# Ranks of the last masks and the places of the last transposes in a two-layer attention and MLP kernel

## Chip, cores and metric

The kernel runs on one core of one Trainium2 chip. The metric is the device time of one execution in microseconds, as the median of several runs. The engines are named as in the profile: PE is TensorE, DVE is VectorE, ACT is ScalarE, POOL is GpSimd, SP is SyncE, which here only issues DMAs.

## What is computed

One sequence of 2048 rows and 640 columns goes twice through the same pair of layers: causal attention with a sliding window of 256 over 32 heads of 20 columns, then an MLP of width 1536 with a squared relu. All is in float32.

```python
def _A_ref(x, wqkv, wo):                      # H = 32, Dh = 20, W = 256
    qkv = ((x @ wqkv).reshape(B, S, 3, H, Dh)).transpose(2, 0, 3, 1, 4)
    q, k, v = qkv[0], qkv[1], qkv[2]
    scores = jnp.einsum("bhqd,bhkd->bhqk", q, k) * (Dh ** -0.5)
    mask = (idx[:, None] - idx[None, :] >= 0) & (idx[:, None] - idx[None, :] < W)
    p = _softmax(jnp.where(mask[None, None], scores, -1e9), axis=-1)
    o = jnp.einsum("bhqk,bhkd->bhqd", p, v)
    return o.transpose(0, 2, 1, 3).reshape(B, S, D) @ wo

def _B_ref(x, w1, b1, w2, b2):                # F = 1536
    h = jnp.einsum("bsd,df->bsf", x, w1) + b1
    r = jnp.where(h > zero, h, zero)
    return jnp.einsum("bsf,fd->bsd", r * r, w2) + b2

x = A_x
x = x + _A_ref(_layernorm(x), A_wqkv, A_wo);  x = x + _B_ref(_layernorm(x), B_w1, B_b1, B_w2, B_b2)
x = x + _A_ref(_layernorm(x), A_wqkv, A_wo);  x = x + _B_ref(_layernorm(x), B_w1, B_b1, B_w2, B_b2)
```

## The kernel before

The rows are cut into units of 256 (two blocks of 128), eight per layer, so sixteen units `u` = 0 to 15 over both layers. Precision comes from splitting operands into a high and a low float16 half: every product of `mm3` runs three matmuls per slice of 128 of the contraction (high by high, high by low, low by high) into one PSUM accumulation.

The heads of a unit are worked in eight groups of four; group `n` counts over all units, so unit 15 has the groups 120 to 127. For each group there are these steps. `max_quad` computes scores for the row maxima, two groups and more ahead. `exp_quad` computes the scores again, transposed, into the six banks of the two `bb` tiles (matmuls at L757); ACT takes six exponentials of them (L779), and POOL sets to zero what lies outside the window with eight masks (`affine_select`, L794 and L798). `pv_quad` multiplies by the values (L828) in three steps, each of which needs its own masks, and ACT copies the result out (L840).

Beside the groups runs the dense work of a neighbouring unit: `stage_qk`, `stage_v`, `stage_o` (the product with `wo`), `stage_y` (normalized rows are transposed by TensorE and evicted as two halves, ACT's cast at L377 and DVE's subtraction at L378) and `stage_f` (the MLP). `stage_f` has a first half of six pairs of tiles of `w1`: a relu on ACT (L1003), a square on POOL (L1007), a cast on ACT (L1010) and a subtraction on DVE (L1013) give the two halves of `hh`. Four buffers hold the relu's output. Its second half has, for each block of rows, chunks of 36 matmuls over `w2`, each ended by an add on DVE (L1042) and, at the end of a block, a store. The accumulations of the dense work take turns in two PSUM banks (`mm_tile`). `load_o` brings the attention's output back from DRAM and divides it by the row sums (`od`, L904 to L914).

The order of the instructions on every engine is written out when the program is built, by a small planner inside the kernel. The dense work is a generator that yields after some 500 ns of matmuls (a piece), with the cost that the kernel assumes for them; `step` advances a clock `now` by that cost. Work for the other engines is posted as jobs with an assumed cost, dependences and a rank `prio`. `post` keeps the list sorted by rank, and within a rank in the order of posting. `pump` takes, again and again, the first job of the list that is ready and can start within `LOOK` = 250 ns of the clock (or another one of the same engine that fits in before it), and emits it. The assumed costs decide only the order; on the chip each engine runs its instructions in that order and waits for semaphores.

Before the change, a mask has rank 1 and a square rank 0, so of two that are due the square is emitted first. In unit 15 the dense work beside the groups is that of unit 14, and the first half of its MLP lies beside the groups 124 to 126. The last lines of the kernel then run the rest: `some(dense, 10e3)` runs pieces of unit 14's MLP for at least 10e3 ns of assumed cost and on to the end of a chunk (until no bank holds an unfinished accumulation), `stage_o(15)` follows, `some(dense, 4e3)` runs the last chunk, and `stage_y(15)` transposes both blocks, five transposes each, into `bb`. Then comes `stage_f(15)`, the last MLP, which has TensorE for itself.

Of the kernel before, what the change touches and what calls it, by code (L numbers as in the profile page):

```python
# [26 lines left out]
NU = NL * NG  # L27
# [4 lines left out]
NQ = H // 4  # L32
# [13 lines left out]
def kernel(ctx: ExitStack, tc: tile.TileContext, x, wqkv, wo, w1, b1, w2, b2, out):  # L46
# [86 lines left out]
    def post(eng, cost, fn, *deps, wait=0.0, prio=1, **kw):  # L133

        j = Job(eng, cost, fn, [d for d in deps if d is not None], now[0] + wait, prio, **kw)
        k = len(pend)
        while k and pend[k - 1].prio > prio:
            k -= 1
        pend.insert(k, j)
        return j  # L140
# [457 lines left out]
    def banks():  # L598
        need(*bbjobs)
        bbjobs.clear()  # L600
        return bb6

    def quarters(u):

        return u % NG != 0
# [131 lines left out]
    def exp_quad(n):  # L737

        u, qd = divmod(n, NQ)
        qt = qts[u]  # L740
        bb = banks()
        whole = not quarters(u) or n == NQ
        steps = steps_of(u)
        if qd % GQ == 0:
            need(rowjobs.pop((u, qd // GQ)))
        pieces = []
        for k, st in enumerate(steps):
            o = 0
            for kb, kt, ko, q0, qn in st:
                w = qn * P  # L750
                for j in range(2):
                    for h in range(0 if whole else 2):
                        a, b = (0, w - 64 * (1 - h)) if kb < 2 else (64 * h, w)

                        def put(e, k=k, kt=kt, ko=ko, q0=q0, j=j, h=h, o=o, a=a, b=b):
                            r, rows = slice(64 * e, 64 * e + 3 * DH + 2), slice(64 * h, 64 * (h + 1))
                            nc.tensor.matmul(bb[e][rows, k, o + a:o + b],  # L757
                                             kt[r, 2 * qd + j, ko + 64 * h:ko + 64 * (h + 1)],
                                             qt[r, 2 * qd + j, q0 * P + a:q0 * P + b], start=True, stop=True,
                                             tile_position=(64 * e, 64 * h))  # L760

                        pieces.append((h, b - a, put))
                    for e in range(2 if whole else 0):
                        r = slice(64 * e, 64 * e + 3 * DH + 2)
                        nc.tensor.matmul(bb[e][:, k, o:o + w], kt[r, 2 * qd + j, ko:ko + P],
                                         qt[r, 2 * qd + j, q0 * P:q0 * P + w], start=True, stop=True)
                    o += w
        by_tiles(pieces)
        now[0] += (870.0 if whole else 763.0) if u % NG else 530.0
        out, masks = [], []  # L770
        for k, st in enumerate(steps):
            pts, ms = [], []
            for e in range(2):
                o = sum(2 * qn * P for _, _, _, _, qn in st)
                box = {}

                def power(k=k, e=e, o=o, box=box):
                    box["pt"] = sb.tile([P, 512], F32, name="pt", tag="pt", bufs=6)
                    nc.scalar.activation(box["pt"][:, :o], bb[e][:, k, :o], AF.Exp, scale=SCALE / (QS * QS))  # L779

                ex = post("A", 50 + 0.834 * o, power, prio=urgency["turn"])
                bbjobs.append(ex)
                o2 = 0
                for kb, kt, ko, q0, qn in st:
                    w = qn * P
                    part = slice(o2, o2 + 2 * w)
                    o2 += 2 * w

                    def mask(box=box, part=part, kb=kb, w=w):
                        pj = box["pt"][:, part].rearrange("p (j n) -> p j n", j=2)  # L790
                        if kb < 2:

                            m = pj[:, :, w - P:w]
                            nc.gpsimd.affine_select(out=m, in_=m, pattern=[[0, 2], [-1, P]],  # L794
                                                    compare_op=ALU.is_gt, fill=0.0, base=0, channel_multiplier=1)
                        else:
                            m = pj[:, :, 0:P]
                            nc.gpsimd.affine_select(out=m, in_=m, pattern=[[0, 2], [1, P]],  # L798
                                                    compare_op=ALU.is_ge, fill=0.0, base=0, channel_multiplier=-1)

                    ms.append(post("G", 375, mask, ex))
                    pts.append((e, kb, q0, qn, box, part))
            out.append(pts)
            masks.append(ms)
        return out, masks
# [168 lines left out]
    def stage_y(u, *between):  # L974

        y2s[u] = y2 = sb.tile([P, 2, KC, T], F16, name="y2", tag="qd", bufs=1)
        ypre[u] = []
        bb = banks() if u == NU - 1 else (None, None)
        for i in range(2):
            y, j = ys.pop((u, i))  # L980
            yield from split_t(y, y2[:, :, :, i * P:(i + 1) * P], j, ypre[u], bb[i])
            for g in between[i:i + 1]:
                yield from g
# [76 lines left out]
    def run(*gs):  # L1060
        s = Stream(chain(*gs))
        while not s.over:
            if s.go() is None and not s.over:
                wait_any(s.want)
# [19 lines left out]
    def some(dense, cost):  # L1084

        while cost > 0 or not all(banks2):
            c = next(dense, None)
            if c is None:
                break
            if not isinstance(c, Want):  # L1090
                cost -= c
            yield c

    def together(ns, ms, dense, cost, share=1.0, whole=True, after=None, pace=0):

        ts = list(turns(ns, ms, pace))
        total = sum(t[0] for t in ts)
        done = part = 0.0
        quad = None
        s = Stream(dense)  # L1100

        def work(part, w):

            nonlocal done
            while True:
                t = when(w) if w else None
                ready = t is not None and t <= now[0]
                if done >= cost * share * part / total and (ready or not w):
                    return
                c = s.go()  # L1110
                if c is not None:
                    done += c
                elif ready or (s.over and not w):
                    return
                else:
                    wait_any(*([w] if w else []), *([s.want] if s.want else []))

        for k, (part_, what, m) in enumerate(ts):
            kind = what and what[0]
            wants = list(bbjobs)  # L1120
            if kind == "s" and what[1] % GQ == 0:
                wants.append(rowjobs[what[1] // NQ, what[1] % NQ // GQ])
            if m is not None:
                wants += [trips[m // NQ, j, m % NQ] for j in range(2)]
            if kind == "v":
                wants += quad[1][0]
            work(part, Want(*wants, bank=kind == "v"))
            if kind == "s":
                quad = exp_quad(what[1])
                for it in late:  # L1130
                    max_out(*it)
                late.clear()
            if m is not None:
                max_quad(m)
                if m % GQ == GQ - 1:
                    if m // NQ > 1:
                        max_cross(m // NQ, m % NQ // GQ)
                    else:
                        late.append((m // NQ, m % NQ // GQ))
            if kind == "v":  # L1140
                pv_quad(what[1], quad)
            if after and k == 0:
                after()
            part += part_
            if what is None:
                work(part, None)
                for it in late:
                    max_out(*it)
                late.clear()
        work(part, None)  # L1150
        if whole:
            while not s.over:
                if s.go() is None and not s.over:
                    wait_any(s.want)
# [73 lines left out]
    while not all(j.end is not None and j.end <= now[0] + LOOK for j in bbjobs):  # L1228
        c = next(rest)
# [5 lines left out]
    for u in range(1, NU):  # L1235
        last = u == NU - 1
        quads, ahead = range(NQ * u, NQ * (u + 1)), range(NQ * u + LEAD, NQ * (u + 1) + LEAD)
        parts, cost, ahead_ln = [], OC + FCST, u + 2 if u + 2 < NU else None
# [10 lines left out]
        dense = chain(*parts, stage_f(u - 1, ahead_ln))  # L1249
        share = 1.0 - KEEP / cost if last else 1.0 - CARRY / cost if u == NU - 2 else 1.0  # L1250
        together(quads, ahead, dense, cost, share, u < NU - 2, after=(lambda: load_o(u - 1, last)) if u > 1 else None, pace=NQ)
    load_o(NU - 1, True)
    run(some(dense, 10e3), stage_o(NU - 1), some(dense, 4e3))
    run(stage_y(NU - 1, iter(()), dense), stage_f(NU - 1))
    need(*list(pend))


# [26 lines left out]
```

## Time and profile before

| what | value |
|---|---|
| median of 3 runs | 1587.85 us (1587.21 to 1589.04) |
| the profiled execution's time | 1588.33 us |
| its span, from the first to the last instruction | 1586.6 us |
| granted TensorE clock, mean | 0.995 |
| busy: PE, DVE, ACT, POOL | 98%, 62%, 46%, 38% |

The span is what the profile's rows add up to. The execution's time is 1.73 us longer and the median of the runs lies 0.48 us under it. Times in the rows count from the span's start. A row of the timeline reads: start, length, engine, line, operation, output and inputs with their shapes, the count of instructions, and in brackets the idle time of the engine ahead of them with what ended it. A row of the chain of waits reads: start, length, engine, tile and line.

### The profile page before, as it was taken

What the parts mean: (1) busy time and instruction counts of PE and PEld (TensorE: products, weight loads), DVE (VectorE), ACT (ScalarE), POOL (GpSimd) and SP (SyncE); (2) the same over time, 40 slices, a digit from 0 to 9 for tenths busy, and PEclk for the clock granted to TensorE, in tenths of its full rate; (3) what the DMA queues carried; (4) which work ended last, traced back from release to release, by engine and by line L of the source; (5) the groups of instructions that cost most, each with busy time, mean ns of one, the idle gap of its engine ahead of it and who ended that gap; (6) DMA issues with size and microseconds to landing.
All of it is one profiled execution on the core that took longest, in us unless ns stands there. A gap on an engine that the chain in (4) does not pass through costs nothing. (4 is left out here: it accounts for less than half of the span.)

```text
span 1586.6 us, 52541 instructions
## 1 busy us (share of the span) xinstructions
PE 1558.1 (98%) x21570; PEld 1168.7 (74%) x21570; DVE 984.7 (62%) x3254; ACT 734.3 (46%) x1593; POOL 600.3 (38%) x1291
## 2 busy tenths in 40 slices
PE   8899999999999999999999999999999999999989
PEld 7666777777777777777777777777778777676767
DVE  8776665666756656565566656657665666756532
ACT  4455545444454444535443453444535345354512
POOL 1233534235253443524324252442525325254512
PEclk9998999999999999999999999999999999999999
DMA  9764343362533525354352534535343343431020
GB/s 272 191 181 117 77 107 86 96 131 55 122 87 103 111 57 127 78 124 90 91 132 64 121 87 110 104 70 128 68 125 83 97 111 69 114 87 58 29 67 18
DMA packets 243353, 160.44 MB, mean 101 GB/s; under 512 B 91176, under 2 KB 226856, under 8 KB 243112
## 3 DMA queue, kind: packets, MB, share of 16 engines
q1 hardware_dynamic: 236744, 147.58, 38.8%
q10 hardware_dynamic: 6368, 9.50, 2.1%
q8 instruction: 169, 2.77, 0.7%
q14 instruction: 72, 0.59, 0.1%
HBM read 84.68 MB, written 52.95 MB: 87 GB/s over the span
## 5 line engine op out<-in xcount | busy, mean ns | idle before, releaser
L779 ACT ACTIVATE pt<-bb 128x512 f32<-128x512 f32 (+1 forms) x736 | 376.0, 600 | 227.0 <-PE bb L757 197.8
L633 DVE CUSTOM_DVE_ANT_0 bb<-bb,maskq 128x320 f32<-128x320 f32 x896 | 409.2, 524 | 86.8 <-PE bb L653 74.6
L794 POOL TENSOR_SCALAR_AFFINE_SELECT pt<-pt 128x256 f32<-128x256 f32 x448 | 188.0, 422 | 563.1 <-ACT pt L779 550.3
L327 PE MATMUL acc<-y,w_s 128*128 128x256 f16 x2880 | 328.3, 273 | 2.5 <-ACT y L377 1.4
L327 PE MATMUL acc<-w_s,hh 128*128 128x320 f16 (+1 forms) x2340 | 326.1, 297 | 0.0
L327 PEld LDWEIGHTS <-w_s 128*128 128x128 f16 x2880 | 276.5, 98 | 54.4 <-issue 18.1
L327 PEld LDWEIGHTS <-hh 128*128 128x128 f16 x2340 | 222.1, 98 | 96.8 <-issue 11.5
L327 PEld LDWEIGHTS <-wq_s 128*128 128x128 f16 x2400 | 229.9, 98 | 46.3 <-issue 13.5
L327 PE MATMUL acc<-yT,wq_s 128*128 128x256 f16 x2250 | 258.6, 273 | 2.2 <-DVE qd L510 0.8
L798 POOL TENSOR_SCALAR_AFFINE_SELECT pt<-pt 128x256 f32<-128x256 f32 x512 | 213.7, 439 | 93.0 <-ACT pt L779 91.6
L1013 DVE TENSOR_TENSOR hh<-r,hh 128x256 f16<-128x256 f32 x192 | 95.1, 517 | 208.8 <-ACT hh L1010 201.8
L828 PE MATMUL pv<-pt,vt 128*32 128x128 f32 (+1 forms) x3840 | 190.9, 331 | 1.2 <-POOL pt L798 1.2
L1007 POOL TENSOR_TENSOR r<-r 128x256 f32<-128x256 f32 x192 | 114.2, 615 | 161.2 <-ACT r L1003 158.8
L840 ACT COPY ot<-pv 128x256 f32<-128x256 f32 x128 | 47.7, 373 | 268.8 <-PE pv L828 268.7
L327 PE MATMUL acc<-wo_s,od 128*128 128x320 f16 x960 | 141.7, 303 | 4.8 <-ACT od L911 3.0
L633 DVE DVE_READ_ACCUMULATOR2_ANT mx<- 128x1 f32 x1024 | 145.1, 142 | 0.0
L828 PEld LDWEIGHTS pv<-pt,vt 128*32 128x32 f32 x3840 | 105.4, 110 | 41.7 <-POOL pt L798 6.5
L327 PE MATMUL acc<-wq_s,yT 128*128 128x320 f16 x900 | 132.0, 299 | 1.4 <-DVE y L378 0.9
L327 PEld LDWEIGHTS <-od 128*128 128x128 f16 x960 | 92.1, 99 | 51.0 <-issue 6.4
L1003 ACT ACTIVATE r<-acc,b1s 128x256 f32<-128x256 f32 x192 | 80.7, 472 | 87.7 <-PE acc L327 86.4
L327 PEld LDWEIGHTS <-yT 128*128 128x128 f16 x900 | 85.7, 98 | 39.3 <-issue 6.7
L364 POOL TENSOR_TENSOR bmv<-bmv,neghalf 128x1 f32<-128x1 f32 x64 | 45.5, 717 | 136.1 <-DVE bmv L358 135.7
(95 smaller groups left out, 1226.3 us busy)
## 6 DMA issues: line engine op xcount, KB each, us to landing
qt<-qk SPq DMA_DIRECT2D x30, 480.0 KB
kt<-qk SPq DMA_DIRECT2D x30, 480.0 KB
qk<-qd SPq DMA_DIRECT2D x17, 640.0 KB
o<-ot SPq DMA_DIRECT2D x256, 42.0 KB
od<-o SPq DMA_DIRECT2D x14, 640.0 KB
qk<-yl SPq DMA_DIRECT2D x13, 640.0 KB
qk<-qd SPq DMA_DIRECT2D x17, 320.0 KB
xt<-in_A_x_dram SPq DMA_DIRECT2D x16, 320.0 KB
```

The costliest lines, as they stand in the source:

```text
L327: nc.tensor.matmul(acc, lhs(a, c), rhs(b, c), start=(k == 0), stop=(k == 3 * nk - 1))
L364: j = post("G", 520, lambda: nc.gpsimd.tensor_tensor(box["mv"][:, 3:4], box["mv"][:, 2:3], neghalf, op=ALU.pow), j, prio=prio)
L633: nc.vector.tensor_tensor_reduce(out=v, in0=v, in1=mask, scale=1.0, scalar=-3.0e38, op0=ALU.add, op1=ALU.max, accum_out=accum[e, w]),
L779: nc.scalar.activation(box["pt"][:, :o], bb[e][:, k, :o], AF.Exp, scale=SCALE / (QS * QS))
L794: nc.gpsimd.affine_select(out=m, in_=m, pattern=[[0, 2], [-1, P]], compare_op=ALU.is_gt, fill=0.0, base=0, channel_multiplier=1)
L798: nc.gpsimd.affine_select(out=m, in_=m, pattern=[[0, 2], [1, P]], compare_op=ALU.is_ge, fill=0.0, base=0, channel_multiplier=-1)
L828: nc.tensor.matmul(pv[32 * jj:32 * (jj + 1), q0 * P:(q0 + qn) * P], vf[:, c:c + 32], pj[:, j, :], start=(k == 0), stop=(k == len(steps) - ...
L840: nc.scalar.copy(ot[:, qd % 2], pv)
L1003: nc.scalar.activation(box["r"], acc[:, f, :], AF.Relu, bias=b1s[:, f0 + f:f0 + f + 1], scale=1.0 / (YS * WS))
L1007: nc.gpsimd.tensor_tensor(box["r"], box["r"], box["r"], op=ALU.mult)
L1013: nc.vector.tensor_sub(hh[:, 1, f, :], box["r"], hh[:, 0, f, :])
```

## The change

The masks of the groups 125, 126 and 127 are posted with rank 0, the squares' rank, instead of 1. The last chunk of unit 14's MLP is cut: a new function `portion` runs pieces until their assumed cost is used up, whether an accumulation is finished or not. After `stage_o(15)` come pieces for 1.8e3 ns, then the transposes of block 0, then pieces for 1.6e3 ns, then the transposes of block 1, then what is left of the chunk, and then `stage_f(15)`. Before, the whole chunk came first, then the transposes of both blocks. No arithmetic is changed.

```diff
-                    ms.append(post("G", 375, mask, ex))
+                    ms.append(post("G", 375, mask, ex, prio=0 if n > NQ * NU - 4 else 1))
...
     def some(dense, cost):
 
         while cost > 0 or not all(banks2):
+            c = next(dense, None)
+            if c is None:
+                break
+            if not isinstance(c, Want):
+                cost -= c
+            yield c
+
+    def portion(dense, cost):
+
+        while cost > 0:
             c = next(dense, None)
             if c is None:
                 break
...
     load_o(NU - 1, True)
-    run(some(dense, 10e3), stage_o(NU - 1), some(dense, 4e3))
-    run(stage_y(NU - 1, iter(()), dense), stage_f(NU - 1))
+    run(some(dense, 10e3), stage_o(NU - 1), portion(dense, 1.8e3))
+    run(stage_y(NU - 1, portion(dense, 1.6e3), dense), stage_f(NU - 1))
     need(*list(pend))
```

## The prediction

> **What bounds the kernel now.** I read the page first, then the chain of waits over the last 107 us, which is where the diff acts: groups 125 to 127 of the last attention unit and the last MLP.
>
> ```profile
> span 1586.6 us, 52541 instructions
> ...
> PE 1558.1 (98%) x21570; PEld 1168.7 (74%) x21570; DVE 984.7 (62%) x3254; ACT 734.3 (46%) x1593; POOL 600.3 (38%) x1291
> ...
> 1496.34 1.95 PE pv L828 x32
> ...
> 1506.91 1.34 POOL r L1007 x2
> 1508.25 0.60 POOL pt L798
> ...
> 1508.89 0.63 PE pv L828 x6
> ...
> 1513.58 1.44 PE pv L828 x32
> ...
> 1526.57 0.49 DVE kt L1042
> 1527.06 0.81 DVE od L914 x2
> ...
> 1541.44 0.49 ACT y L377
> ...
> 1541.95 0.57 DVE y L378
> ...
> 1542.54 1.04 ACT y L377 x3
> ...
> 1544.22 39.37 PE acc L327 x359
> ```
>
> TensorE is busy for 98% of the span, so almost nothing but its holes can be won, and the chain leaves TensorE (the rows that are not PE) in three places after 1500 us. Around 1506 to 1508.9 it goes through ACT's relu, two squares on POOL and one mask on POOL (L798): `pv` of group 126 waits for its last mask, which stands behind two squares. At 1526.6 it goes through DVE's add and `od`. At 1541.4 to 1544.2 it goes through ACT's and DVE's evictions of the transposes (L377, L378). The diff touches the first and the third. The views of single engines show the sizes:
>
> ```profile
> 1506.23 1.49 PE L828 MATMUL pv<-pt,vt 128*32 128x256 f32 x26
> 1508.89 0.63 PE L828 MATMUL pv<-pt,vt 128*32 128x256 f32 x6 [1.18 <-POOL pt L798]
> 1509.46 0.75 PE L757 MATMUL bb<-qt,kt 62*64 62x192 f16 x32
> ...
> 1535.80 5.05 PE L327 MATMUL acc<-w_s,hh 128*128 128x320 f16 x36
> 1540.69 1.26 PE L391 MATMUL bb<-ident,xt 128*128 128x128 f32 x10
> 1543.35 0.27 PE L327 MATMUL acc<-y,w_s 128*128 128x256 f16 x1 [1.40 <-ACT y L377]
> 1544.22 1.03 PE L327 MATMUL acc<-y,w_s 128*128 128x256 f16 x8 [0.60 <-DVE y L378]
> ```
>
> From the first transpose (1540.69) to the second matmul of the last MLP (1544.22) pass 3.53 us, though the ten transposes and one matmul need about 1.2.
>
> **The masks, part by part.** The edit adds and removes no instruction: in groups 125 to 127 eight masks each get rank 0 instead of 1 in the planner's list, so that among POOL jobs due at one moment the one posted first goes first, not the square.
>
> ```profile
> 1492.76 1.37 POOL L794 TENSOR_SCALAR_AFFINE_SELECT pt<-pt 128x256 f32<-128x256 f32 x3 [1.07 <-ACT pt L779]
> 1494.27 1.18 POOL L1007 TENSOR_TENSOR r<-r 128x256 f32<-128x256 f32 x2
> 1495.40 0.41 POOL L798 TENSOR_SCALAR_AFFINE_SELECT pt<-pt 128x256 f32<-128x256 f32 x1
> ...
> 1496.12 1.49 POOL L798 TENSOR_SCALAR_AFFINE_SELECT pt<-pt 128x256 f32<-128x256 f32 x3
> ...
> 1505.83 0.76 POOL L798 TENSOR_SCALAR_AFFINE_SELECT pt<-pt 128x256 f32<-128x256 f32 x2
> 1506.91 1.34 POOL L1007 TENSOR_TENSOR r<-r 128x256 f32<-128x256 f32 x2 [0.31 <-ACT r L1003]
> 1508.21 0.63 POOL L798 TENSOR_SCALAR_AFFINE_SELECT pt<-pt 128x256 f32<-128x256 f32 x1
> ...
> 1513.08 1.12 POOL L798 TENSOR_SCALAR_AFFINE_SELECT pt<-pt 128x256 f32<-128x256 f32 x3
> ```
>
> ```profile
> 1496.34 1.01 DVE L1013 TENSOR_TENSOR hh<-r,hh 128x256 f16<-128x256 f32 x2 [3.75 <-ACT hh L1010]
> ...
> 1506.17 1.03 DVE L1013 TENSOR_TENSOR hh<-r,hh 128x256 f16<-128x256 f32 x2 [4.55 <-ACT hh L1010]
> ```
>
> The planner's clock settles order only, never a time here. Its constants are those of the code, in ns: exponential 477, relu 360, square 571, mask 375, 165 from the end of a job on ACT to one that needs it; a job is put in order once it can start within 250 of the clock, the lower rank first.
>
> *Group 126.* Before the last step of `pv` the planner needs mask 8. Counted from the end of the scores, eight dense pieces of 545 and two steps of `pv` of 480 put its clock at 5320. The first pair's relu starts after two pieces, its squares at 1090 + 360 + 165 = 1615, five masks follow, and mask 7 ends at 1615 + 2 x 571 + 5 x 375 = 4632. The second pair's relu starts after eight pieces, its square at 4360 + 360 + 165 = 4885. So mask 8 and that square are both due; today the square's rank puts both squares first, after the change mask 8 goes first. Earlier nothing flips: after four pieces (2180), when the second square is put, mask 3 can't start before 1090 + 720 + 477 + 165 = 2452, 272 off and not within 250. So POOL runs mask 8 straight behind mask 7: the two masks at 1505.83 take 0.76, so it starts at about 1506.55 and ends after 0.41 (the mask at 1495.40) to 0.63 (the row at 1508.21), at 1506.96 to 1507.18, not 1508.84. An unbroken `pv` takes 1.44 in the chain (group 127); group 126 spans 1509.46 - 1506.23 = 3.23, to the start of the scores of 127. Gain: 3.23 - 1.44 = 1.79 at most. Its last six matmuls last 1509.46 - 1508.89 = 0.57 up to those scores, so mask 8 is due at 1506.23 + 1.44 - 0.57 = 1507.10, and its later end costs 0.1. I take **1.7**.
>
> A subtraction on DVE (L1013, x2, 1506.17 to 1507.20) runs beside that mask. Beside such subtractions the three masks at 1496.12 took 1.49, against 0.41 for one alone and 0.76 for two; so a mask is stretched by about 0.2, which the 1507.18 holds. Were it to wait out the subtraction instead, it would run from 1507.20 to 1507.61, 0.5 late, and the gain would be 1.3 (rival 3). [...] The three masks at 1496.12 speak for a stretch: with two waits of 0.4 each they would have taken 2.0 instead of 1.49.
>
> *Group 125.* The fourth mask goes ahead of the two squares (today: after them, 1495.40). The second square still goes before mask 5, by the same 272 ns. POOL's work is the same, but between mask 3 and the first square it idles about 0.14 (1492.76 + 1.37 = 1494.13 to 1494.27), which mask 4 now fills. `pv` of 125 takes 1.95 instead of 1.44; from these 0.51 the last mask wins at least 0.14 and at most all. I take **0.2**: POOL stays the limit.
>
> *Group 127.* No squares compete with its masks, but the last two squares now end about 0.2 later while the scores come 1.7 earlier, so their casts to `hh` come before the exponentials on ACT:
>
> ```profile
> 1507.71 0.40 ACT L1010 CAST hh<-r 128x256 f16<-128x256 f32 x1 [0.52 <-POOL r L1007]
> ...
> 1510.31 3.04 ACT L779 ACTIVATE pt<-bb 128x512 f32<-128x512 f32 x6 [0.33 <-PE bb L757]
> ```
>
> Scores start at 1507.7; six exponentials start 0.85 after their scores now (1509.46 to 1510.31), that would be 1508.5. The second square ends at about 1508.3, its cast takes 0.41 and ends at 1508.9, so exponentials and masks come 0.36 late. The masks end at 1513.08 + 1.12 = 1514.20 and `pv` needs the last at about 1513.58 + 1.44 - 0.57 = 1514.4, a slack of 0.2 that the 0.36 overdraws. **-0.2**; ends 0 and -0.4. The number of dense pieces between scores and `pv` stays (six pieces of four matmuls, 24): they wait for the planned end of the exponentials, which moves with the scores. The `od` wait at 1526.6 also stays: its cover, 84 matmuls after `pv`, is the same.
>
> Masks together: 0.2 + 1.7 - 0.2 = 1.7, ends 1.0 and 2.3.
>
> **The transposes, part by part.** The edit moves matmuls of the last chunk of the previous MLP (36 at 0.136, from 5.05 less the tail of 0.16). A piece is four matmuls of 136 by the code, 544 ns: 1.8e3 takes four pieces (16 matmuls), 1.6e3 three (12), 8 are left. The transposes' bank is `bb`, the chunk's a `mm` bank, so nothing has to be finished first. Beside the 0.136 no switching cost shows: the first transpose begins at 1540.69 = 1535.80 + 36 x 0.136, and ten take 1.1 without their tail. Two more switches I bound at 0 to 0.1 each.
>
> The normalized rows must be ready:
>
> ```profile
> 1534.37 0.60 DVE L366 TENSOR_SCALAR xt<-x,bmv 128x640 f32<-128x640 f32 x1
> ...
> 1538.38 0.61 DVE L366 TENSOR_SCALAR xt<-x,bmv 128x640 f32<-128x640 f32 x1 [0.66 <-POOL bmv L364]
> ...
> 1543.60 0.89 DVE L378 TENSOR_TENSOR y<-bb,y 128x384 f16<-128x384 f32 x2 [0.23 <-ACT y L377]
> ...
> 1541.44 0.48 ACT L377 CAST y<-bb 128x384 f16<-128x384 f32 x1 [10.17 <-PE bb L391]
> ...
> 1541.86 0.37 SPq L952 DMA_DIRECT2D xt<-in_B_b_dram  x1
> ```
>
> `y` of block 0 ends at 1534.97, of block 1 at 1538.99. In the old clock, new order: 16 matmuls to 1537.98; five transposes (0.55) to 1538.53; 12 matmuls to 1540.16; five transposes to 1540.71; 8 matmuls to 1541.80. Block 1 has 1.2 us of slack. On DVE, block 1's normalization is planned before block 0's subtraction, so it isn't delayed. Eviction of block 1, by today's intervals: ACT starts 0.75 after the first transpose (1540.69 to 1541.44): 1540.91; 0.48 and then 0.57 on DVE (the chain's first) end at 1541.97. The first matmul may start at 1541.80, the second at 1542.0 instead of 1544.22: **2.2**. The second half (256 columns for 384, so about two thirds of 0.48 and of 0.57) ends at about 1542.7; the eleventh matmul, the first that asks for it whole, comes at 1541.8 + 1.2 = 1543.0 (0.109 each: eight span 1.03 in the row at 1544.22, one 0.27). Ends: 2.3, if nothing waits; 1.0, if ACT's copy gets its signal only behind the eight matmuls that follow.
>
> What else moves: the chunk's add on DVE and its store now come after the second evictions, at about 1542, and free a bank that the MLP asks for 3.3 us later. The load of `b2` (SP, 1541.86 now) needs only block 0's buffer and is planned ahead of that store; even behind it, at 1542.5, it lands some 0.6 later than now while POOL's squares are due 2.2 earlier. That delays squares by up to 1.5 us, against the two pairs (6.5 us) that pass before a relu needs their buffer. No cost. After that the 39.37 us of TensorE are the same.
>
> **Sum.** 1.7 + 2.2 = 3.9 us. The profiled execution's span is 1586.6 and its time 1588.33; that becomes 1584.4. The median of the runs, 1587.85, lies 0.48 under it, and becomes **1584.0**.
>
> **Rivals.**
> 1. *The ranks do nothing, or what they give is lost at once* (the planner's order differs from my working, or group 127 loses what 126 wins): the transposes alone, 1587.85 - 2.2 = 1585.7. Against it: both jobs are due by hundreds of ns, only the rank decides. 0.11.
> 2. *The evictions still come last.* A signal behind the eight matmuls, or DVE's add ahead of the subtraction, leaves 1.0 or less of the transposes: 1587.85 - 1.7 - 0.8 = 1585.4. For it: ACT's second copy waits for DVE today (1542.54), so these two engines take turns for a reason that isn't in the source. 0.09.
> 3. *The mask waits out the subtraction* rather than being stretched: gain in 126 is 1.3, so 1587.85 - 3.5 = 1584.4. 0.10.
> 4. *Slower: masks that wait for exponentials hold up the squares.* POOL works in order. If a whole group of masks went before a pair of squares, relus would run out of their four buffers. The squares at 1494.27 have until the relu two pairs later:
>
> ```profile
> 1503.06 0.84 ACT L1003 ACTIVATE r<-acc,b1s 128x256 f32<-128x256 f32 x2
> ```
>
> With subtractions done at about 1497.4, that is 5.7 us of slack; only a delay beyond it costs. Held behind group 126's last mask (1508.84) the squares, casts and subtractions end at about 1510.9, and that relu is 7.9 us late; net of the transposes' 2.2 the time is 1593.6. Against it: the planner keeps every job within 250 ns of its clock, so a square waits for a mask or two. 0.05.
>
> **How the numbers follow.** Forecast 0.62, rivals 0.11, 0.09, 0.10, 0.05, and 0.03 unnamed. 0.2% (3.2 us, about what a measurement of this kernel can tell from no change) lies inside the forecast's reach: with terms of 1.0 to 2.3 and 2.0 to 2.3, about one in eight of its cases wins less. Faster by over 0.2%: 0.55 of the forecast's 0.62, 0.08 of rival 3, 0.01 unnamed, 0.64. Slower: rival 4 and 0.01, 0.06. Same: 0.30. The range takes the best ends of both parts (4.6) from the lowest run (1587.21), 1582.6, drawn in to 1582.9, and rivals 1 and 2 with half a microsecond of spread between runs, 1586.2.
>
> **What would show it.** Right: POOL's order in group 126 is eight masks before the two squares and `pv` of 126 is one block of about 1.45 us; in the chain, five transposes, 12 matmuls, five transposes, 8 matmuls, and the last MLP starts without a wait over 0.3. Wrong: two squares still ahead of the last mask; `pv` of 127 broken by over 0.4; TensorE waiting for L366 ahead of the second five transposes, or over 0.5 for L377 or L378 behind them.

## The result and the profile after

| | median of the runs | runs |
|---|---|---|
| before | 1588.38 us (1587.21 to 1589.04) | 6 |
| after | 1581.57 us (1580.44 to 1582.38) | 6 |

The ratio is 0.996, with a 95% interval of 0.9949 to 0.9971. The change wins 6.8 us where 3.9 were forecast. The profiled execution took 1582.29 us, 6.04 less than that of before, and its span is 6.1 us shorter.

Two lines of the page of the kernel after:

```profile
span 1580.5 us, 52541 instructions
...
PE 1555.9 (98%) x21570; PEld 1168.6 (74%) x21570; DVE 985.7 (62%) x3254; ACT 733.6 (46%) x1593; POOL 600.4 (38%) x1291
```

The chain of waits of the kernel after, from group 126 to the last matmul (start, length, engine, tile and line):

```profile
1504.10 1.52 PE pv L828 x32
...
1509.67 1.49 PE pv L828 x32
1511.16 11.53 PE acc L327 x84
...
1522.72 0.49 DVE kt L1042
1523.21 0.81 DVE od L914 x2
...
1524.07 10.22 PE acc L327 x74
1534.29 0.55 PE bb L391 x5
1534.84 1.63 PE acc L327 x12
1536.46 0.55 PE bb L391 x5
1537.01 40.52 PE acc L327 x368
```

Two of the three places at which the chain left TensorE are gone. `pv` of group 126 stands in it unbroken, and from the transposes to the last matmul nothing but TensorE is in it: five transposes, 12 matmuls, five transposes, and then 368 matmuls in one piece, the 8 left of the chunk and the last MLP. The wait for DVE's add and `od` is as it was. On the timelines of TensorE and POOL, kernel after, this reads:

```profile
1505.55 0.75 PE L757 MATMUL bb<-qt,kt 62*64 62x192 f16 x32
...
1511.10 11.58 PE L327 MATMUL acc<-w_s,hh 128*128 128x320 f16 x84
...
1524.07 8.05 PE L327 MATMUL acc<-wo_s,od 128*128 128x320 f16 x58 [1.11 <-DVE od L914]
...
1534.13 0.71 PE L391 MATMUL bb<-ident,xt 128*128 128x128 f32 x5
...
1536.85 1.25 PE L327 MATMUL acc<-w_s,hh 128*128 128x320 f16 x8
1537.93 7.27 PE L327 MATMUL acc<-y,w_s 128*128 128x256 f16 x64
```

```profile
1503.27 0.41 POOL L794 TENSOR_SCALAR_AFFINE_SELECT pt<-pt 128x256 f32<-128x256 f32 x1
1503.63 1.30 POOL L798 TENSOR_SCALAR_AFFINE_SELECT pt<-pt 128x256 f32<-128x256 f32 x3
1504.91 1.34 POOL L1007 TENSOR_TENSOR r<-r 128x256 f32<-128x256 f32 x2
```

On POOL the last four masks of group 126 run on without a square between, and the two squares follow. The first matmul of the last MLP (1537.93) has no wait ahead of it. The second starts 0.05 us behind the end of DVE's eviction, 0.24 after the first where the next ones are 0.11 apart. DVE's row, and TensorE's from the second matmul on:

```profile
1537.56 0.56 DVE L378 TENSOR_TENSOR y<-bb,y 128x384 f16<-128x384 f32 x1 [0.76 <-ACT y L377]
...
1538.17 7.15 PE L327 MATMUL acc<-y,w_s 128*128 128x256 f16 x64
```

**Where the 6.1 us of span lie.** No instruction ahead of the scores of group 124 differs between the two kernels. The row in which those scores start splits each profile into a "head" and a "rest"; it stands at 1480.79 before and at 1478.96 after (the next two fences: TensorE, before and after).

```profile
1480.79 0.96 PE L757 MATMUL bb<-qt,kt 62*64 62x192 f16 x32
```

```profile
1478.96 0.96 PE L757 MATMUL bb<-qt,kt 62*64 62x192 f16 x32
```

The head is 1.83 us shorter with the same instructions in it. The rest goes from 1586.6 - 1480.8 = 105.8 to 101.6: 4.2 us. Between the same starts of rows, before and after, the rest divides so:

| stretch of the rest | before | after | gain | predicted |
|---|---|---|---|---|
| scores of 125 to scores of 126 | 9.95 | 9.59 | 0.36 | 0.2 |
| scores of 126 to scores of 127 | 8.39 | 6.67 | 1.72 | 1.7 |
| scores of 127 to the 84 matmuls | 5.48 | 5.55 | -0.07 | -0.2 |
| the 84 matmuls to the end of `stage_o` | 20.86 | 20.85 | 0.01 | 0 |
| from there to the second matmul of the last MLP | 8.42 | 6.22 | 2.20 | 2.2 |

Group 124 takes 10.33 in both profiles, and what follows the second matmul of the last MLP 42.36 and 42.37, so the parts make up the 4.2. The stretches that the prediction costed came out as costed, 4.2 for 3.9, and what it missed lies elsewhere.

### The profile page after: what moved, and what is told of

Read it like the earlier page. It is cut to its first block, busy times and chain, and to the rows that moved or that the text cites. A ratio compares the mean times of both kernels' runs of the same rounds, so it can differ in the third digit from the quotient of the medians.

```text
span 1580.5 us, 52541 instructions
## 1 busy us (share of the span) xinstructions
PE 1555.9 (98%) x21570; PEld 1168.6 (74%) x21570; DVE 985.7 (62%) x3254; ACT 733.6 (46%) x1593; POOL 600.4 (38%) x1291
```

## Experiments

The first four tell three theories apart. Theory 1: the part that differs wins about 4.2 us, and the rest of the difference is the head, which scatters from execution to execution. Theory 2: an edit of the program moves the head for good. Theory 3: of the edits only the moved transposes do. The times of the three groups below come from three further chips, each beside its own runs of the kernel before (32, 28 and 15 of them; medians 1587.19, 1586.83 and 1587.11). "Mean against before" is the difference of the means of the runs with its standard error.

**The masks alone** (e1): of the change only the rank.

```diff
-                    ms.append(post("G", 375, mask, ex))
+                    ms.append(post("G", 375, mask, ex, prio=0 if n > NQ * NU - 4 else 1))
```

> The mask ranks alone; the end stays as before. I split each profile at the start of the scores of group 124 (1480.79 us before, 1478.96 after), ahead of which no instruction differs: the head, and the rest (105.8 us before, 101.5 after). Theory of the parts (each edit gives what the two traces show at its place): rest 105.8 - 2.0 = 103.8. Rival (the parts share a gain): 105.0 or more. For the head, theory 1 (it scatters from execution to execution): anywhere from 1477 to 1482, and the median of the runs 1586.4, 2.0 under the kernel before, within a microsecond. Theory 2 (any edit of the program moves the head for good, since it is placed anew in memory): a head near 1479, the median 1584 or less. Theory 3 (only the moved transposes do it): head near 1480.8.

**The transposes alone** (e2): `portion` and the last two calls of `run`, without the rank.

```diff
-    run(some(dense, 10e3), stage_o(NU - 1), some(dense, 4e3))
-    run(stage_y(NU - 1, iter(()), dense), stage_f(NU - 1))
+    run(some(dense, 10e3), stage_o(NU - 1), portion(dense, 1.8e3))
+    run(stage_y(NU - 1, portion(dense, 1.6e3), dense), stage_f(NU - 1))
```

> The cut chunk and the moved transposes alone; masks rank 1 as before. Theory of the parts: rest 105.8 - 2.25 = 103.5. Rival: 104.5 or more. Head: theory 1, anywhere from 1477 to 1482, median of the runs 1586.1; theory 2, head near 1479 and the median 1583.7 or less; theory 3, the same numbers as theory 2 here and those of theory 1 without scatter in the masks alone.

**An unused function** (e3): the kernel before with `portion` defined and never called, so that all instructions are the same.

```diff
+    def portion(dense, cost):
+
+        while cost > 0:
...
```

> The kernel before with the function portion added and not called: every engine gets the same instructions in the same order, only line numbers move by ten. Rest: 105.8 by every theory. Head: theory 1, anywhere from 1477 to 1482 and the median of the runs within 1 us of the kernel before; theory 2, placed like the kernel before, 1480.8 and the same time within 0.5; if the median lies 2 us or more lower with the same instructions, something outside the instructions sets the head.

**The changed kernel again** (e4), with no edit to it, on the chip of e1 to e3.

> The changed kernel once more. Rest: 101.5 within 0.2. Theory 1 (the head scatters): its median against the kernel before on the same chip is 4.3 us lower within 1 us, so near 1584, not 6.8. Theory 2 (the head is faster for good in this program): 6 to 7 us lower, 1581 to 1582, head 1477 to 1479.

| kernel | median | ratio (95%) | mean against before | head | rest |
|---|---|---|---|---|---|
| e1, masks | 1584.33 | 0.9984 (0.9976 to 0.9993) | -2.84 ± 0.44 | 1480.09 | 103.78 |
| e2, transposes | 1584.65 | 0.9985 (0.9976 to 0.9995) | -2.82 ± 0.76 | 1478.18 | 103.63 |
| e3, unused function | 1589.35 | 1.001 (0.9999 to 1.002) | +1.39 ± 0.59 | 1480.37 | 107.49 |
| e4, after again | 1581.31 | 0.9967 (0.9955 to 0.9979) | -5.52 ± 0.87 | 1479.86 | 101.64 |

In the rests the parts add up: 105.8 - 103.78 = 2.0 for the masks and 2.2 for the transposes, 4.2 together, as in the changed kernel. The heads do not go by the program: the kernel before stands at 1480.79 and, profiled again below (e8), at 1477.70, the changed kernel at 1478.96, 1479.86 and 1479.17 (after, e4 and e10). So theories 2 and 3 get no support from them.

The times of the runs are less clear, and no theory had all of them right. The medians of e1, e2 and e4 lie 1.4 to 2.7 under those of theory 1; e4's is where theory 2 had it. And e3, which changes no instruction, is 1.4 slower in the mean and 2.2 in the median. Part of this goes with the granted clock, whose mean is on record for every run. The 75 runs of the kernel before take 1588.3 us on the average where it is 0.996 and 1586.5 where it is 0.998, about 1 us for each 0.001. On the chip of e1 to e4 it is 0.9970 in the kernel before, 0.9977 in e1 and in e2, 0.9975 in e4 and 0.9960 in e3. By that slope, and as an estimate, it accounts for 0.7 of the 2.8 us of e1 and of e2, 0.5 of e4's 5.5 and 1.0 of e3's 1.4. Why the clock of e3's runs is the lower one isn't shown.

But e3's rest is 1.7 us longer than that of the kernel before, with the same instructions, and this was in no theory. Its place is a single row of the chain (e3; the row of before, in the prediction, has 39.37 for the same 359 matmuls):

```profile
1543.82 41.03 PE acc L327 x359
```

The windows of TensorE show why, for the kernel before and for e3 (stretch, its length, busy time of TensorE with the count of matmuls, granted clock, DMA share, GB/s). The stretches are 3.41 us long and laid through the steps of the granted clock that the profiles record; in that of before it stands at half, for one, from 48.93 to 52.34.

```profile
1540.56:1543.97 3.41, 1.66 (x14) 1.00 0.42 146
1543.97:1547.39 3.42, 3.17 (x30) 1.00 0.16 51
```

```profile
1540.88:1544.29 3.41, 1.41 (x13) 1.00 0.68 163
1544.29:1547.70 3.41, 3.41 (x19) 0.50 0.10 34
```

The hole behind the last transposes, 1.40 + 0.60 us of waits, fell whole into one window of e3: TensorE was busy 1.41 of 3.41 us, and the next window ran at half clock, which costs the 41.03 - 39.37 = 1.66 us. In the profile of before the same hole left 1.66 us busy in its window, and the clock stayed at 1.00. So the hole that the change removes may have a second price, which the profile of before happens not to show. The next runs ask this.

**The hole bare** (e5): the kernel before with the whole chunk ahead of `stage_o(15)`, so that nothing is between `stage_o` and the transposes, and the holes there are longer.

```diff
-    run(some(dense, 10e3), stage_o(NU - 1), some(dense, 4e3))
-    run(stage_y(NU - 1, iter(()), dense), stage_f(NU - 1))
+    run(some(dense, 20e3), stage_o(NU - 1))
+    run(stage_y(NU - 1, iter(()), iter(())), stage_f(NU - 1))
```

> The kernel before with the whole last chunk run ahead of stage_o(15), so that nothing covers the normalization of block 1 and the evictions behind it: TensorE idles some 3.4 us ahead of block 1's transposes and 1.8 us behind them. By waits alone: 6.0 us from the end of stage_o to the second matmul of the last MLP instead of 3.5, and the od wait of 1.1 to 1.5 gone, since the chunk covers it: rest 105.8 + 2.5 - 1.3 = 107.0, and no stage of the clock at half after 1540 us. By the theory that such a hole costs the clock too (the granted clock fell to a half for 3.41 us right behind the 2.0 us of waits at this place in the kernel with the unused function, and its last MLP took 41.03 us instead of 39.37): one stage of 3.41 us or two at half behind the hole, rest 108.7 or 110.4, and the last MLP 41.0 us or longer.

**The same holes, filled** (e6): matmuls of the identity, whose result nobody reads, stand in them.

```diff
+    def filled(n):
+        spin(n)
+        yield 0.0
+
     run(some(dense, 20e3), stage_o(NU - 1))
-    run(stage_y(NU - 1, iter(()), iter(())), stage_f(NU - 1))
+    run(stage_y(NU - 1, filled(15), filled(3)), stage_f(NU - 1))
```

> The same, with 15 and 3 matmuls of the identity (0.22 us each, results unused) put into the two holes; all other orders equal. They end before the wait does. By waits alone: the same rest as without them, within 0.3. By the clock theory: no stage at half, the last MLP 39.4 us, rest 107.0, so 1.7 us or 3.4 us below the kernel without them.

**Both `od` ahead of the add** (e7): a version meant to beat the changed kernel. It is the changed kernel with the add of unit 14's third chunk posted 1300 ns later, so that DVE does both subtractions of `od` (L914) ahead of it and the wait of 1.11 us in front of `stage_o` goes.

```diff
-        hj = []
+        hj, late_add = [], 1300.0
...
-  lambda wait: jobs.append(post("D", 88 + n, add, *b2j[2 * i:2 * i + 2], wait=wait, prio=0)))
+  lambda wait: jobs.append(post("D", 88 + n, add, *b2j[2 * i:2 * i + 2],
+                            wait=wait + late_add * ((u, i, c0) == (NU - 2, 1, 0)), prio=0)))
```

> The changed kernel with the add of unit 14's third chunk put in order 1.3 us later by the planner, so that DVE does both od subtractions of stage_o's first block ahead of it: by today's rows they end at 1526.7 in the clock of the kernel before, not 1527.85, and the wait of TensorE shrinks from 1.1 plus a first broken start to 0.3. Rest 101.6 - 1.2 = 100.4. Rival: od's data come last anyway (its casts end at 1526.04), and the wait only changes its name: 101.3 or more.

**The kernel before again** (e8), with no edit, as one more profile of it.

> The kernel before once more, for the scatter of its head and of its end. Rest 105.8 or, if the clock falls behind the waits at 1542 to 1544, 107.5; head between 1477 and 1482. If the head is a property of the program, it stands at 1480.8 within 0.3; if it scatters by execution, the six heads seen so far (1478.2 to 1480.8) say that it may be anywhere there.

**Before, with the hole filled** (e9): six matmuls of the identity behind the last transposes, in the wait of 1.40 us.

```diff
+    def filled(n):
+        yield from dense
+        spin(n)
+        yield 0.0
+
-    run(stage_y(NU - 1, iter(()), dense), stage_f(NU - 1))
+    run(stage_y(NU - 1, iter(()), filled(6)), stage_f(NU - 1))
```

> The kernel before with six matmuls of the identity (1.3 us, results unused) in the 1.4 us hole behind its last transposes; the wait itself stays. Seen so far with that hole: rest 105.8 and, where the clock fell to a half behind it, 107.5 (two of three profiles of these orders). Clock theory: rest 105.8 and the last MLP 39.4 us in this kernel, and the mean of its runs 0.5 to 1.1 us under that of the kernel before. Rival (the stage at half comes by chance, whatever TensorE does): it may be seen here too, and the means are equal.

**The changed kernel a third time** (e10), and **e7 once more** (e11), both with no edit, on the chip of e9.

> The changed kernel, third look. Rest 101.6, no stage at half behind 1530 us, head anywhere from 1477.5 to 1481. By the sum of parts (4.2 in the rest, 0.8 for a stage at half in about half of the executions before) the mean of its runs lies 5.0 under the kernel before on this chip, within 0.9; if the 6.8 of the first comparison is the program's own, 6.0 or more.

> The changed kernel with the late add (od first), beside the changed kernel on one chip. Rest 100.3 and 1.3 us under the changed kernel in the mean, if the heads are alike; their scatter of some 1 us per execution leaves 0.5 either way.

| kernel | median | ratio (95%) | mean against before | head | rest |
|---|---|---|---|---|---|
| e5, bare | 1591.16 | 1.0025 (1.0015 to 1.0035) | +3.80 ± 0.57 | 1480.66 | 108.59 |
| e6, bare and filled | 1588.59 | 1.001 (1.0001 to 1.0019) | +1.53 ± 0.56 | 1478.82 | 107.25 |
| e7, `od` first | 1581.71 | 0.9969 (0.9957 to 0.998) | -5.36 ± 0.79 | 1479.73 | 100.30 |
| e8, before again | 1586.91 | 1.0001 (0.9992 to 1.001) | -0.11 ± 0.38 | 1477.70 | 107.46 |
| e9, before filled | 1586.22 | 0.9995 (0.9986 to 1.0004) | -0.94 ± 0.47 | 1478.18 | 105.83 |
| e10, after a third time | 1582.31 | 0.9965 (0.9953 to 0.9978) | -5.24 ± 0.44 | 1479.17 | 101.66 |
| e11, `od` first again | 1582.26 | 0.9965 (0.9953 to 0.9978) | -5.17 ± 0.59 | 1479.23 | 101.28 |

**What e5 and e6 show.** Windows of TensorE in e5 and in e6, and the row of the last MLP in the chain of each:

```profile
1538.06:1541.48 3.42, 1.93 (x16) 1.00 0.08 29
1541.48:1544.89 3.41, 0.98 (x6) 1.00 0.25 67
1544.89:1548.30 3.41, 2.81 (x15) 0.50 0.02 5
```

```profile
1541.48:1544.89 3.41, 2.81 (x24) 1.00 0.00 0
1544.89:1548.30 3.41, 3.41 (x34) 1.00 0.00 0
```

```profile
1545.54 40.70 PE acc L327 x359
```

```profile
1543.70 39.37 PE acc L327 x359
```

In e5 TensorE was busy 0.98 us in a window, and the next ran at half clock. In e6, where the needless matmuls stand, it was busy for 2.81 and 3.41 us of the same two windows, the clock stayed at 1.00, and the same 359 matmuls take 39.37 instead of 40.70. (The 40.70 is less than the 41.0 expected, since the window at half clock was busy for only 2.81 us.) The two kernels wait for the same evictions: from the first transpose to the second matmul of the last MLP pass 6.26 us in e5 and 6.25 in e6. Yet the one with more matmuls is the shorter by 108.59 - 107.25 = 1.34 us in the profiles, and 1.33 of that is the row above. In the means of the runs it is the shorter by 2.3, of which what goes beyond 1.3 isn't separated from the scatter. The runs' mean clocks, 0.9955 and 0.9967, differ by 0.0012, and one window at half clock is 0.5 x 3.41 / 1589 = 0.0011 of an execution's mean: so the runs too speak for one such window.

**What e8, e9 and e1 show of the hole as it is.** Windows of e8, e9 and e1 around the hole:

```profile
1538.56:1541.97 3.41, 1.41 (x12) 1.00 0.70 189
1541.97:1545.38 3.41, 3.41 (x18) 0.50 0.03 8
```

```profile
1538.27:1541.69 3.42, 2.76 (x24) 1.00 0.35 136
```

```profile
1536.62:1540.03 3.41, 2.61 (x22) 1.00 0.14 55
1540.03:1543.45 3.42, 2.22 (x19) 1.00 0.64 142
```

The kernel before, profiled again, has the stage at half clock (1.41 us busy, as in e3). In e1, which keeps the hole, the hole fell across the edge of two windows (2.61 and 2.22 busy) and cost nothing but its wait (its 359 matmuls took 39.37). So where the windows' edges lie against the hole differs from execution to execution: of the four profiles that keep the hole as it is (before, e1, e3, e8) two have the stage. The six with the transposes moved (after, e2, e4, e7, e10, e11) and the two with a filled hole (e6, e9) have none there. At 1.66 us in half of the executions it is worth about 0.8 us on the average; that is an estimate from two in four. The runs of e9, where only the clock can win, give 0.94 ± 0.47; its ratio's interval still holds 1.

**What e7 and e11 show.** The wait went, in one profile wholly and in the other by half. The chain of e7 has no DVE between `pv` of group 127 and the transposes; on e11's TensorE a wait of 0.49 is left:

```profile
1511.94 21.84 PE acc L327 x160
```

```profile
1523.98 8.05 PE L327 MATMUL acc<-wo_s,od 128*128 128x320 f16 x58 [0.49 <-DVE od L914]
```

DVE's reciprocal ahead of `od` waits for a DMA (`rs<-o`), 0.20 us in e7 and 1.17 in e11, and its data came later in e11 than in e7, seen from `stage_o`: it starts 4.00 us ahead of it in e7 (1519.29 to 1523.29) and 3.24 in e11 (1519.81 to 1523.05). The rest is shorter than that of the changed kernel by 1.3 and by 0.4, but in the runs of one chip (e10 and e11) the means are 1582.06 and 1582.13. The version isn't shown to beat the change.

## Why the prediction was right and wrong

**Group 126 (right).** Eight masks stand ahead of the two squares, `pv` is one block of 1.52 us in the chain, and 1.72 us are won for 1.7.

**Group 125 (right in kind, a little small).** Mask 4 fills POOL's gap. The gain is 0.36, inside the bounds of 0.14 and 0.51; `pv` went from 1.95 to 1.58.

**Group 127 (right).** The casts did come ahead of the exponentials, which start 1506.60 - 1505.55 = 1.05 after the scores instead of 0.85, so 0.2 late and not 0.36 (ACT, kernel after):

```profile
1505.97 0.72 ACT L1010 CAST hh<-r 128x256 f16<-128x256 f32 x2
1506.60 3.03 ACT L779 ACTIVATE pt<-bb 128x512 f32<-128x512 f32 x6
```

The slack of 0.2 took almost all of it: 0.07 were lost for 0.2.

**Transposes (right).** 2.20 for 2.2, in the order of 16, 5, 12, 5 and 8. The first eviction starts 0.74 after the first transpose, as the interval of the kernel before said, and the normalized rows are not waited for. The one eviction that is waited for, by about 0.13, is the one that the prediction had: the second matmul at 1542.0, 0.2 behind the first. Of the two parts on their own, e1 and e2 gave 2.0 and 2.2 in the rest.

**Rivals 1, 2 and 4 (did not come) and 3 (came in kind, not at its price).** The ranks worked, no eviction holds the last MLP up beyond what was forecast, and the squares that stand behind the masks hold up nothing. For rival 3, here are single instructions of DVE and POOL in the kernel after, in order of time, and last a subtraction with no mask beside it:

```profile
1503.97 0.70 DVE L1013 TENSOR_TENSOR hh<-r,hh 128x256 f16<-128x256 f32 x1 [4.55 <-ACT hh L1010]
1503.99 0.40 POOL L798 TENSOR_SCALAR_AFFINE_SELECT pt<-pt 128x256 f32<-128x256 f32 x1
1504.35 0.59 POOL L798 TENSOR_SCALAR_AFFINE_SELECT pt<-pt 128x256 f32<-128x256 f32 x1
1504.59 0.62 DVE L1013 TENSOR_TENSOR hh<-r,hh 128x256 f16<-128x256 f32 x1
1504.91 0.77 POOL L1007 TENSOR_TENSOR r<-r 128x256 f32<-128x256 f32 x1
...
1506.41 0.42 DVE L1013 TENSOR_TENSOR hh<-r,hh 128x256 f16<-128x256 f32 x1 [1.20 <-ACT hh L1010]
```

Undisturbed, a mask takes 0.41, a subtraction 0.42 and a square 0.61 (the one at 1505.64). So the first subtraction is 0.28 too long, mask 8 behind it 0.18, the second subtraction 0.20 and the square 0.16. Counted back from their ends by the undisturbed lengths, these four began their own work at 1504.25, 1504.53, 1504.79 and 1505.07. The other engine's instruction ahead of each ended at 1504.39, 1504.67, 1504.94 and 1505.21: later by 0.14 or 0.15 each time. So in these rows the two engines take turns, instruction by instruction, as if each waited until 0.14 or 0.15 us before the other's recorded end. That is a reading of these rows; what makes the engines wait isn't shown.

What rival 3 had wrong is the price. By this reading mask 8 waited 0.18 for the rest of one subtraction, and not 0.5 for both, since the second subtraction in its turn waited for the mask. The forecast took about the same 0.2 from the rows of the kernel before and called it a stretch: its size was right and, by this reading, its mechanism was not. Its argument from the three masks at 1496.12 counted two waits of 0.4 each; taken singly, the second and the third of them lasted 0.59 and 0.58 against 0.41, so they waited 0.18 and 0.17.

**The first step that failed: "After that the 39.37 us of TensorE are the same."** In the profiles of before and after they are. But for the kernel before, this number depends on the execution: with the hole in it, the last MLP takes 39.37 or 41.03. The hole was priced by its wait alone. It also puts a stage of 3.41 us at half clock behind itself in some executions, two profiles in four, and the change takes that away with the hole. With about 0.8 for it the forecast would have been 4.7, and by the measured rest 5.0. The two further comparisons on other chips gave 5.5 ± 0.9 and 5.2 ± 0.4. Of the 2.9 us by which the measured 6.8 exceeds the forecast 3.9, the costed terms hold 0.3 and this step about 0.8; the other 1.8 are taken up below.

**The second: the range.** Its lower end, 1582.9, takes the best ends of both parts from the lowest of three runs and is drawn in from there, and its upper end allows "half a microsecond of spread between runs". The medians of the changed kernel on all three chips, 1581.57, 1581.31 and 1582.31, lie under it, and the single runs of the kernel before on the three further chips lie between 1584.24 and 1594.76. Over the 13 profiles, all with the same instructions up to the scores of group 124, the head lies between 1477.70 and 1480.79, and the profile of before is the longest of them. It has five windows at half clock in its head and the changed kernel's has four; e2 and e9, with one each (the mean clock of both executions is 0.999), have heads of 1478.18. The order between isn't strict: e8 has two (its mean clock, 0.997, makes three with the one at 1541.97), and the shortest head. In the pair of the result the heads part early. The same stretch, before and then after (busy times of all engines, clock, DMA share):

```profile
45.00:60.00 15.00, 12.62 (x126) 8.48 (x124) 8.84 (x38) 6.90 (x16) 4.24 (x10) 0.89 0.61 176
```

```profile
45.00:60.00 15.00, 14.17 (x155) 10.84 (x155) 12.16 (x49) 10.05 (x22) 4.24 (x10) 1.00 0.64 188
```

TensorE did 1.5 us more work there in the kernel after, at a clock of 1.00 instead of 0.89, with the program unchanged. The 1.83 between the two heads lies inside the 3.1 us over which the heads scatter, so it can't be put down to the change.

**What stays open.** Of the 6.8 us of the first comparison, 4.2 are the two edits and about 0.8 the clock. The other 1.8 lie in the size of the head's scatter for single executions, but a mean over six runs on each side should leave less of it. The two other chips do not repeat it, nor is it shown that it was chance. It sits on the side of the kernel before: its median is 1588.38 in the first comparison and 1586.83 to 1587.19 on the other chips, while that of the changed kernel is 1581.57 there and 1581.31 and 1582.31 elsewhere.

## What to carry to other kernels

The hole in this kernel, which keeps TensorE busy, had two prices: its waits, 1.40 and 0.60 us, and, in two of four profiles, 1.66 us by the clock behind it. The clock fell where the hole left TensorE busy for 1.41 of 3.41 us (e3, e8), and stayed where it left 1.66 (before) or 2.22 and 2.61 us (e1). Elsewhere both are to be measured. Count the windows at the place, for one profile shows only one of its possible phases. Split two profiles at the first instruction that differs before a gain is read from them: what lies ahead of it is scatter, and it gives the width that the range needs. Where no useful work can be moved into such a hole, even needless matmuls can pay (e6 against e5, by 1.34 us in the profiles).

## What the runs showed of the hardware

In the profile of before the granted clock steps at 48.93, 52.34, 72.83, 76.24, 117.20 and 127.44 us, between 1.00 and 0.50: 3.41 us or a whole multiple of it apart. These windows of 3.41 us are not tied to the program's start: for the same program, and counted from the span's start, one begins at 1540.56 in the profile of before and one at 1538.56 in that of e8, 2.00 us apart. In the last 50 us the windows behind those in which TensorE was busy 0.98 (e5) and 1.41 us (e3, e8), 29% and 41%, ran at half clock, and behind 1.66 us (before, 49%), 1.93 (e5), 2.22 and 2.61 (e1), 2.76 (e9) and 2.81 (e6) the clock stayed. Of the windows at full clock in the profiles of before and after, from the first record of the clock (4.56 and 4.65) to the last matmul, the five with 1.44, 1.48 and 1.35 us busy (before, from 45.52, 69.42 and 113.78) and 1.48 and 1.26 (after, from 66.09 and 110.47) had one at half clock behind them, and the others, with 1.66 us or more, had not. Busy time doesn't divide all that were seen: behind the 1.93 us of e5 the clock stayed, and behind 1.99 us, earlier in the same execution, it fell. Windows of e5 and then of e9, early in the kernel, with the same instructions there:

```profile
32.79:36.20 3.41, 1.99 (x19) 1.00 1.04 204
36.20:39.61 3.41, 3.41 (x14) 0.50 1.14 256
```

```profile
33.00:36.41 3.41, 2.00 (x18) 1.00 0.99 199
36.41:39.82 3.41, 3.19 (x29) 1.00 1.15 251
```

So TensorE's busy time in the rows alone doesn't tell when the clock falls, and what else counts stays open. Of the windows that were themselves at half clock, those with 2.05 and 2.50 us busy (before, from 117.20 and 120.61) and with 2.23 and 2.31 (after, from 113.88 and 117.29) had another at half clock behind them; behind 2.81 us (e5, from 1544.89) and behind the five that were busy throughout (before, from 48.93, 72.83 and 124.02; after, from 69.50 and 120.70) the clock was back at 1.00.

In e3 and e8 the window ahead of the one at half clock wasn't idle: it holds 3.41 - 1.41 = 2.00 us of waits, with TensorE busy for the other 41%. One window at half clock cost 1.66 us with all of it busy (e3, e8) and 1.33 with 2.81 us busy (e5).
